# Wide feature maps and zero-weight filler matmuls in a kernel planned by its own scheduler

## The chip, the cores and the metric

The program runs on one core of a Trainium2 chip. Times are device microseconds of that core; the span that a profile shows, from the first to the last instruction, is some 2 us shorter.

## The reference

Four residual layers over 2048 tokens of width 512 with 32 heads of 16. Layers 0 and 2 are "memory layers": causal attention within four segments of 512 tokens, plus a linear-attention memory that runs over the segments. Layers 1 and 3 are plain attention over all 2048 tokens.

```python
phi = lambda t: jnp.where(t > 0, t + 1.0, jnp.exp(t))
for s in range(N):                                   # memory layer, N = 4 segments
    logits = jnp.einsum('bhqd,bhkd->bhqk', qs, ks) * scale + mask
    a_dot = jnp.einsum('bhqk,bhkd->bhqd', _softmax(logits, axis=-1), vs)
    pq = phi(qs)
    a_mem = jnp.einsum('bhld,bhde->bhle', pq, M) / (jnp.einsum('bhld,bhd->bhl', pq, z)[..., None] + 1e-06)
    outs.append(g * a_mem + (1.0 - g) * a_dot)
    pk = phi(ks)
    M = M + jnp.einsum('bhld,bhle->bhde', pk, vs)
    z = z + jnp.einsum('bhld->bhd', pk)
# ... layers: x + A(ln(x)), x + B(ln(x)), x + A(ln(x)), x + B(ln(x)); A = memory layer, B = full attention
```

Nearly all the work is the exponential of the softmax. Most of it runs on ACT (three 128x512 score tiles at a time, from three PSUM banks, while PE fills the three others). Some runs on DVE by a polynomial, four tiles at a time.

## The kernel before

The program is built by a planner in Python. It keeps a modelled time for each engine and puts down, step by step, what PE is to do next: a group of scores, a product with V, or a dense projection that some thread waits for. The order on every engine is fixed by this plan. Its numbers are tuned by stage: `TUNE` lists them by the count of exponentials planned so far, and `PAT` says how units of two layers are interleaved. The planner also models the PE clock. It counts activity in windows of 3.41 us and adds `CF * cold` to a matmul when it thinks the clock is half.

```python
def clock(self, t, work):                      # the planner's model of the PE clock
    w = int(t / HAM_W)                         # HAM_W = 3.4133
    if w > self.win:
        self.warm = w == self.win + 1 and self.work >= HAM_T     # HAM_T = 5.0
        self.win, self.work = w, 0.0
    self.work += work                          # 1.0 dense 512 columns, 0.14 a score tile, 0.16 a product with V
...
# end of the planning loop: PE has nothing ready until `to`
    if KEEP and self.acc_open and t + d <= tc + KEEP_D and (...) <= sc.lately() < KEEP and (...):
        self.keep_warm()                       # KEEP = 0.0 here: never
        continue
    sc.t["pe"] = to
...
# memory layers, one chunk of 512 columns at a time: masked query, feature map, masked query
sc.add("dve", lambda e: e.tensor_scalar(qe, qo, self.parm[:, 0:1], None, op0=ALU.mult), ...)
if L % 2 == 0 and s > 0:
    yield from self.g_phi(L, s, qo, self.b_q[z][1][c], self.ph[:, c, :], self.b_ph[c], f"q{c}")
o = sc.add("dve", lambda e: e.tensor_scalar(qo, qo, self.parm[:, 1:2], None, op0=ALU.mult), ...)
...
def g_phi(...):                                # phi(t) = max(t, 0) + min(exp(t), 1)
    o = sc.add("act", lambda e: e.activation(dst, src, ACT.Exp), ..., cost=0.65)
    o = sc.add("dve", lambda e: e.tensor_scalar(dst, dst, 1.0, None, op0=ALU.min), ..., cost=0.29)
    o = sc.add("dve", lambda e: e.scalar_tensor_tensor(res, src, 0.0, dst, op0=ALU.max, op1=ALU.add), ..., cost=0.71)
...
# layer norm of a segment: four tiles through two buffers, each transposed by a DMA
xn, bxn = self.xn[:, i % 2, :], self.b_xn[i % 2]
o = sc.add("dve", ... e.tensor_scalar(xn, xt, mu, r1, op0=ALU.subtract, op1=ALU.mult) ...)
o = self.dma_T(self.xT[:, s, :, i * 128:(i + 1) * 128], xn, [bxn], [self.b_xT[s][i]], f"lT{L}_{s}{i}")
```

The softmax here doesn't subtract the row's maximum and nothing guards it: scores larger than these inputs give would overflow.

## Time and profile before

| | before |
|---|---|
| time, median of the first 3 runs | 2082.6 us |
| ACT busy / PE busy / DVE busy | 96% / 82% / 79% |
| mean PE clock | 0.649 |
| ACT's own work (steps of its instructions, end to end) | 1976.3 us |
| ACT's loss up to the 110th exponential (191 us) | 44.4 us |
| loss from the 110th to the 1100th (191 to 1495 us) | 43.9 us |
| loss after that | 9.5 us |
| after ACT's last instruction | 8.1 us |

"Loss" is used throughout as in the prediction: the distance from the end of one ACT instruction to the end of the next, less that instruction's own step (1.343 us for 1536 columns from PSUM, 0.490 for 512, 0.515 for 512 from SBUF). Work, loss and the rest after the last instruction add up to the span. I call the three stretches start-up, middle and end. "Warm" and "cold" stand for the full and the half clock of PE.

The costliest groups of the page (line, engine, operation, tiles and shapes, count | busy us and mean ns | idle before it and what ended that idle) show the same bound from PE's side:

```profile
L1135 ACT ACTIVATE pT<-ps 128x1536 bf16<-128x1536 f32 (+2 forms) x1525 | 1957.3, 1458 | 66.1 <-PE ps L1128 57.4
L1128 PE MATMUL ps<-q,kB 32*128 32x512 bf16 x3660 | 699.6, 546 | 256.3 <-ACT pT L1135 248.3
```

PE waits 248 us for ACT to free banks ahead of its scores; ACT waits 57 us for scores.

### The profile page before, as it was taken

The numbers are of one execution on the slowest core, as the hardware profiler recorded it, in microseconds if no ns is written. First come the engines' busy times: TensorE is split into PE (matmuls) and PEld (weight loads), VectorE is DVE, ScalarE is ACT, GpSimd is POOL, SyncE is SP. The second block draws the span as 40 slices with busy tenths as digits, with TensorE's granted clock in tenths as the row PEclk, the third lists the DMA queues.
The fourth block names the chain that finished last, engine by engine and source line by source line (L and its number), as shares of the span: only waits on it lengthen the run. The fifth ranks groups of instructions, "written<-read, shape, count | busy, mean of one in ns | idle before, by whom it ended". The sixth has DMA issues, their size and how long they took to land.

```text
span 2082.3 us, 41423 instructions
## 1 busy us (share of the span) xinstructions
PE 1705.9 (82%) x17296; PEld 592.2 (28%) x17382; DVE 1645.9 (79%) x2492; ACT 1990.4 (96%) x1615; POOL 253.3 (12%) x564
## 2 busy tenths in 40 slices
PE   6768888888878888788787788888888888888887
PEld 2222221112311121212222223213444444444443
DVE  6886758887678688787878577688789988898986
ACT  6879899999999999999999999999999999999997
POOL 4542410001400000211013103100000000000000
PEclk9679897557565675557776797675655555555555
DMA  4210100001000000001010100100000000000000
GB/s 122 51 32 11 28 15 1 1 1 21 7 16 1 11 11 1 1 1 21 1 21 1 21 11 2 21 1 2 14 5 4 4 14 4 5 4 15 6 4 12
DMA packets 75467, 27.31 MB, mean 13 GB/s; under 512 B 68112, under 2 KB 74768, under 8 KB 75280
## 3 DMA queue, kind: packets, MB, share of 16 engines
q1 hardware_dynamic: 74176, 23.62, 5.2%
q8 instruction: 136, 2.23, 0.5%
q10 hardware_dynamic: 1104, 1.05, 0.2%
q14 instruction: 51, 0.42, 0.1%
HBM read 6.30 MB, written 2.10 MB: 4 GB/s over the span
## 4 chain that ended last, share of the span: by engine, by line
ACT 49%; PE 29%; issue 11%; DVE 7%; POOL 2%; DMA 1%; SPq 0%; ACTq 0%; DVEq 0%; POOLq 0%
ACT pT L1135 48%; PE ps L1128 13%; PE ps L625 6%; PE ps L1379 5%; PE ps L1397 4%; POOL pT L1158 2%; PE ps L1267 1%; DMA xT<-xn 1%; DVE lnst L662 1%; DVE T L1517 0%; DVE tokk L786 0%; ACT ph L780 0%; DVE ot L919 0%; SPq L444 0%; DVE db L1325 0%
## 5 line engine op out<-in xcount | busy, mean ns | idle before, releaser
L1135 ACT ACTIVATE pT<-ps 128x1536 bf16<-128x1536 f32 (+2 forms) x1525 | 1957.3, 1458 | 66.1 <-PE ps L1128 57.4
L1128 PE MATMUL ps<-q,kB 32*128 32x512 bf16 x3660 | 699.6, 546 | 256.3 <-ACT pT L1135 248.3
L1270 DVE TENSOR_SCALAR dz<-ps 128x512 int32<-128x512 f32 x436 | 301.0, 691 | 156.8 <-PE ps L1267 143.6
L1128 PEld LDWEIGHTS ps<-q,kB 32*128 32x128 bf16 x3660 | 131.4, 97 | 701.5 <-ACT pT L1135 656.1
L1158 POOL TENSOR_SCALAR_AFFINE_SELECT pT<-pT 128x256 bf16<-128x256 bf16 (+2 forms) x516 | 223.8, 463 | 613.4 <-ACT pT L1135 611.9
L1397 PE MATMUL ps<-pT,vB 128*17 128x512 bf16 x2216 | 278.7, 507 | 0.7 <-DVE q L640 0.5
L1267 PE MATMUL ps<-q,kB 32*128 32x512 bf16 x436 | 250.0, 573 | 0.0
L1379 PEld LDWEIGHTS ps<-vB,pT 128*128 128x128 bf16 x5776 | 181.1, 104 | 160.8 <-issue 157.6
L1379 PE MATMUL ps<-vB,pT 128*128 128x17 bf16 x5776 | 213.4, 177 | 0.7 <-ACT pT L1135 0.4
L1128 PE MATMUL ps<-q,kA 32*128 32x512 bf16 (+3 forms) x1024 | 122.4, 385 | 47.7 <-ACT pT L1135 45.6
L1307 DVE TENSOR_SCALAR df<-dz 128x2048 f16<-128x2048 uint16 x109 | 134.0, 1229 | 2.4
L1397 PEld LDWEIGHTS ps<-pT,vB 128*17 128x17 bf16 x2216 | 51.0, 89 | 187.0 <-issue 176.5
L1314 DVE TENSOR_SCALAR db<-dz 128x2048 int16<-128x2048 int16 x80 | 97.8, 1222 | 1.6 <-PE ps L1397 1.6
L1517 DVE STREAM_TRANSPOSE T<-ps 128x512 f32<-128x512 f32 x94 | 66.6, 709 | 15.3 <-PE ps L1397 14.7
L625 PE MATMUL ps<-xT,wB 128*128 128x512 bf16 x228 | 70.4, 429 | 7.4 <-issue 3.9
L625 PE MATMUL ps<-xT,wA 128*128 128x512 bf16 x238 | 68.7, 412 | 8.1 <-issue 2.1
L991 DVE TENSOR_TENSOR x_tok<-x_tok,ps 128x512 bf16<-128x512 bf16 x60 | 41.0, 686 | 41.6 <-PE ps L625 41.3
L1319 DVE TENSOR_TENSOR tokk<-tokk,df 128x2048 f16<-128x2048 f16 x58 | 70.7, 1219 | 0.7
L1323 DVE TENSOR_TENSOR tokk<-tokk,df 128x2048 f16<-128x2048 f16 x58 | 70.7, 1218 | 0.6
L1128 PEld LDWEIGHTS ps<-q,kA 32*128 32x128 bf16 x1024 | 29.9, 99 | 125.7 <-ACT pT L1135 110.9
L680 DVE TENSOR_SCALAR xn<-x_tok,lnmv,lnr 128x512 bf16<-128x512 bf16 x60 | 24.5, 429 | 50.3 <-DMA xT<-xn 49.4
L1325 DVE TENSOR_TENSOR db<-db,dz 128x2048 int16<-128x2048 int16 x51 | 62.8, 1231 | 1.2
(128 smaller groups left out, 1513.2 us busy)
## 6 DMA issues: line engine op xcount, KB each, us to landing
x_tok<-in_A_x_dram SPq DMA_DIRECT2D x14, 128.0 KB, 2.7
wB<-in_B_wqkv_dram SPq DMA_DIRECT2D x4, 384.0 KB, 3.9
out_dram<-x_tok SPq DMA_DIRECT2D x3, 512.0 KB, 3.0
xT<-xn SPq DMA_TRANSPOSE x60, 2.4
wA<-in_A_wk_dram SPq DMA_DIRECT2D x1, 512.0 KB, 7.7
wA<-in_A_wq_dram ACTq DMA_DIRECT2D x1, 512.0 KB, 7.9
wA<-in_A_wv_dram SPq DMA_DIRECT2D x1, 512.0 KB, 8.8
woA<-in_A_wo_dram SPq DMA_DIRECT2D x1, 512.0 KB, 7.5
```

What stands on the lines that cost most here:

```text
L625: return self.sc.add("pe", lambda e: e.matmul(out, lhsT, rhs, start=start, stop=stop), reads=reads, bank_ops=[(bank, "w", alloc)], emit=la ...
L1128: sc.add("pe", (lambda out, lhsT, rhs: lambda e: e.matmul(out, lhsT, rhs, start=True, stop=True))(out, lhsT, rhs), reads=reads, bank_ops=[ ...
L1135: o = sc.add("act", lambda e: e.activation(dst, src, ACT.Exp, scale=float(SCALE)), writes=[self.b_pT[s0 + i] for i in range(n)], bank_ops= ...
L1158: om = sc.add("pool", (lambda ap, pat: lambda e: e.affine_select(ap, ap, pattern=pat, compare_op=ALU.is_ge, fill=0.0, base=0, channel_mult ...
L1267: sc.add("pe", lambda e: e.matmul(out, lhsT, rhs, start=True, stop=True), reads=reads, bank_ops=[(bank, "w", alloc)], emit=True, name="SX" ...
L1270: o = sc.add("dve", lambda e: e.tensor_scalar(dst, out, float(EXP_C * 65536.0), -126.0 * 65536.0, op0=ALU.mult, op1=ALU.max), writes=[self ...
L1307: o = dv(lambda e: e.tensor_scalar(F, lo, 2.0 ** -16, -0.5, op0=ALU.mult, op1=ALU.add), bz, bF, "dF", 1.24)
L1314: o = dv(lambda e: e.tensor_scalar(E, hi, 128.0, 16256.0 + 53.0, op0=ALU.mult, op1=ALU.add), bz, bE, "dE", 1.24)
L1319: o = dv(lambda e: e.tensor_tensor(Pz, Pz, F, ALU.mult), bF + bP, bP, "dP2", 1.24)
L1323: o = dv(lambda e: e.tensor_tensor(Pz, Pz, F, ALU.mult), bF + bP, bP, "dP4", 1.24)
L1379: op = sc.add("pe", (lambda o0, w, v, first: lambda e: e.matmul(self.ps[:, o0:o0 + 17], w, v, start=first, stop=True, skip_group_check=Tru ...
L1397: sc.add("pe", (lambda out, v, rhs, start, stop: lambda e: e.matmul(out, v, rhs, start=start, stop=stop, skip_group_check=True))(out, v, r ...
```

## The change

Its intent: (1) where ACT is the bound, save fixed costs by mapping two chunks in one instruction; (2) where PE would idle, issue a matmul with zero weights that adds nothing, or one into a free bank that nobody reads, so that the PE clock stays at full speed and projections take half the time. New planner numbers and orders come with it.

```diff
-PAT = ["AAAAAAAA", "ABABABABBBABAAABBA", "BAAABBBAAAAA", "AAAAABABABAB", "AAAABABABBAA", "BBABAABAAA"]
+PAT = ["AAAAAAAA", "ABABABABBBABAAABBA", "BAAABAABABAA", "AAAAABABBBAA", "AAABBBABAAAA", "BBABABAAAA"]
+HALF = True
-    (0, {'CF': 0.829, 'PB': 0.02, 'DX_AHEAD': 0.5, ...}),
+    (0, {'CF': 1, 'PB': 0.026, 'DX_AHEAD': 0.696, ..., 'KEEP': 0.0, 'KEEP0': 3.0, 'KEEP_D': 0.0}),
+    (110, {'MMC': 0.205, 'KEEP': 9.0}),
     ... (all rows of TUNE are new)
+    (1100, {'DX_AHEAD': 0.664, 'MMC': 0.2, 'KEEP': 0.0, 'KEEP_D': 0}),
-        self.et = sb("et", [P, 512], bf)
+        self.et = sb("et", [P, 1024], bf)
+        if HALF and L % 2 == 0 and s > 0:
+            h = c // 2                       # waits for both chunks of the half, then
+            ...                              # mask, map (wide=True) and mask over 1024 columns
-            for c in range(NCH):
+            for h in range(2):
                 yield ("t", o.t_end, 0.0)
-                ... g_phi(L, s, tk, self.b_tokk[c], et, self.b_et, f"k{c}", tk, self.b_tokk[c])
+                tk = self.tokk[:, 2 * h:2 * h + 2, :].rearrange("p i f -> p (i f)")
+                ... g_phi(L, s, tk, self.b_tokk, self.et[:, :], self.b_et, f"k{h}", tk, self.b_tokk, wide=True)
-            if KEEP and self.acc_open and t + d <= tc + KEEP_D and (...) and self.pvu and self.pvu[0]["L"] <= KEEP_L:
-                self.keep_warm()
+            if KEEP and t + d <= tc + KEEP_D and (0.0 if sc.warm else KEEP0) <= sc.lately() < KEEP and self.keep_warm():
     def keep_warm(self):
+        if self.acc_open:
+            bank, alloc, start = self.acc_bank, self.acc_alloc, False
+        else:
+            bank = self.free_bank()
+            if bank.t_free + 0.12 > sc.t["pe"]:
+                return False
+            alloc, start = self.new_alloc(), True
+        sc.add("pe", lambda e: e.matmul(self.ps[:, bank.col0:bank.col0 + 512], self.zw[:, :], self.wA[:, 0, 0:512], start=start, stop=start,
+                                        skip_group_check=True), ..., name="D", cost=0.215, cold=0.2133, work=1.0)
+        return True
```

(Cut: a small constant tile now lives in the scratch buffer `et`.)

More of the change, by code (lines that the diff above doesn't have):

```diff
@@ L54 @@
 DX3 = 1
+HALF = True
 TUNE = [
-    (0, {'CF': 0.829, 'PB': 0.02, 'DX_AHEAD': 0.5, 'DX_SLACK': 4.776, 'DX_LEAD': 69, 'DVE_AHEAD': 4.525, 'MAXPV': 3, 'RATE': 0.606, 'MMC': 0.22, 'LN_G': 3, 'PV0': 0.371, 'DX3': 1}),
-    (110, {'CF': 0.849, 'RATE': 0.472, 'MMC': 0.229}),
-    (220, {'MMC': 0.213, 'PV0': 0.365}),
-    (330, {'LN_G': 2}),
-    (440, {'DVE_AHEAD': 2.5}),
-    (660, {'PB': 0.022}),
-    (880, {'PB': 0.026, 'RATE': 0.4}),
-    (990, {'MMC': 0.2, 'PV0': 0.324}),
-    (1100, {'CF': 1, 'PB': 0.025, 'DX_AHEAD': 0.676, 'LN_G': 3}),
-    (1210, {'PB': 0.036, 'DX_LEAD': 64, 'DVE_AHEAD': 3.61}),
-    (1320, {'DX_SLACK': 5.687}),
-    (1430, {'PB': 0.035, 'DX_LEAD': 53, 'DVE_AHEAD': 3.961, 'MAXPV': 2}),
+    (0, {'CF': 1, 'PB': 0.026, 'DX_AHEAD': 0.696, 'DX_SLACK': 4.776, 'DX_LEAD': 69, 'DVE_AHEAD': 4.525, 'MAXPV': 3, 'RATE': 0.581, 'MMC': 0.22, 'LN_G': 3, 'PV0': 0.371, 'DX3': 1, 'KEEP': 0.0, 'KEEP0': 3.0, 'KEEP_D': 0.0}),
+    (110, {'MMC': 0.205, 'KEEP': 9.0}),
+    (220, {'DX_LEAD': 64}),
+    (440, {'CF': 0.912, 'PB': 0.029}),
+    (550, {'DX_AHEAD': 0.5}),
+    (660, {'PB': 0.023, 'KEEP0': 1.467, 'KEEP_D': 0.003}),
+    (770, {'PB': 0.024, 'RATE': 0.679}),
+    (880, {'MAXPV': 4, 'KEEP_D': 0.03}),
+    (990, {'DX_AHEAD': 0.603, 'MMC': 0.207, 'KEEP0': 1.866}),
+    (1100, {'DX_AHEAD': 0.664, 'MMC': 0.2, 'KEEP': 0.0, 'KEEP_D': 0}),
+    (1210, {'PB': 0.02, 'DX_AHEAD': 0.749, 'DVE_AHEAD': 5.31, 'PV0': 0.368}),
+    (1320, {'CF': 1}),
+    (1430, {'DX_AHEAD': 1.301}),
 ]
@@ L346, in alloc @@
         self.gm = sb("gm", [P, NCH, 136], bf)
-        self.bmf = sb("bmf", [P, 136], f32)
+        self.bmf = self.et[:, 0:272].bitcast(f32)
         self.parm = sb("parm", [P, 2], f32)
@@ L397, in alloc @@
         self.b_gm = B("gm")
-        self.b_bmf = B("bmf")
+        self.b_bmf = self.b_et
         self.b_parm = B("parm")
@@ L769, in g_q @@
             return
+        if HALF and L % 2 == 0 and s > 0:
+            h = c // 2
+            key = ("cnt_q", L, s, h)
+            self.cnt[key] = self.cnt.get(key, 0) + 1
+            if self.cnt[key] < 2:
+                return
+            cs = slice(2 * h, 2 * h + 2)
+            qo, qe = self.q[:, z, 1, cs, :], self.q[:, z, 0, cs, :]
+            bo, be = self.b_q[z][1][cs], self.b_q[z][0][cs]
+            o = sc.add("dve", lambda e: e.tensor_scalar(qe, qo, self.parm[:, 0:1], None, op0=ALU.mult),
+                       reads=bo + [self.b_parm], writes=be, name=f"qm{L}{s}0", cost=0.45)
+            yield from self.g_phi(L, s, qo, bo, self.ph[:, cs, :], self.b_ph[cs], f"q{c}", wide=True)
+            o = sc.add("dve", lambda e: e.tensor_scalar(qo, qo, self.parm[:, 1:2], None, op0=ALU.mult),
+                       reads=bo + [self.b_parm], writes=bo, name=f"qm{L}{s}1", cost=0.45)
+            for x in (2 * h, 2 * h + 1):
+                self.set_ev(("q", L, s, x), o.t_end)
+            return
         sc.add("dve", lambda e: e.tensor_scalar(qe, qo, self.parm[:, 0:1], None, op0=ALU.mult),
@@ L776, in g_q, with g_phi @@
         self.set_ev(("q", L, s, c), o.t_end)
-    def g_phi(self, L, s, src, bsrc, dst, bdst, nm, res=None, bres=None):
+    def g_phi(self, L, s, src, bsrc, dst, bdst, nm, res=None, bres=None, wide=False):
         sc = self.sc
-        o = sc.add("act", lambda e: e.activation(dst, src, ACT.Exp), reads=[bsrc], writes=[bdst], name=f"phe{L}{s}{nm}", cost=0.65)
+        bsrc, bdst = ([x] if isinstance(x, Buf) else list(x) for x in (bsrc, bdst))
+        o = sc.add("act", lambda e: e.activation(dst, src, ACT.Exp), reads=bsrc, writes=bdst, name=f"phe{L}{s}{nm}", cost=1.07 if wide else 0.65)
         yield ("t", o.t_end, 0.0)
-        o = sc.add("dve", lambda e: e.tensor_scalar(dst, dst, 1.0, None, op0=ALU.min), reads=[bdst], writes=[bdst],
-                   name=f"phm{L}{s}{nm}", cost=0.29)
+        o = sc.add("dve", lambda e: e.tensor_scalar(dst, dst, 1.0, None, op0=ALU.min), reads=bdst, writes=bdst,
+                   name=f"phm{L}{s}{nm}", cost=0.43 if wide else 0.29)
         if res is None:
             res, bres = dst, bdst
-        o = sc.add("dve", lambda e: e.scalar_tensor_tensor(res, src, 0.0, dst, op0=ALU.max, op1=ALU.add), reads=[bsrc, bdst],
-                   writes=[bres], name=f"phs{L}{s}{nm}", cost=0.71)
+        o = sc.add("dve", lambda e: e.scalar_tensor_tensor(res, src, 0.0, dst, op0=ALU.max, op1=ALU.add), reads=bsrc + bdst,
+                   writes=bres if isinstance(bres, list) else [bres], name=f"phs{L}{s}{nm}", cost=1.24 if wide else 0.71)
         return o
@@ L862, in g @@
             self.set_ev(("phk", L, s))
-            for c in range(NCH):
+            for h in range(2):
                 yield ("t", o.t_end, 0.0)
-                tk = self.tokk[:, :, c * 128:(c + 1) * 128]
-                et = self.et[:, :].rearrange("p (i f) -> p i f", i=4)
-                o = yield from self.g_phi(L, s, tk, self.b_tokk[c], et, self.b_et, f"k{c}", tk, self.b_tokk[c])
+                tk = self.tokk[:, 2 * h:2 * h + 2, :].rearrange("p i f -> p (i f)")
+                o = yield from self.g_phi(L, s, tk, self.b_tokk, self.et[:, :], self.b_et, f"k{h}", tk, self.b_tokk, wide=True)
             for c in range(NCH):
@@ L1846, in run @@
             tc = min([x for x in (rs, rp, rx) if x is not None], default=to)
-            if KEEP and self.acc_open and t + d <= tc + KEEP_D and (0.0 if sc.warm else KEEP0) <= sc.lately() < KEEP and self.pvu and self.pvu[0]["L"] <= KEEP_L:
-                self.keep_warm()
+            if KEEP and t + d <= tc + KEEP_D and (0.0 if sc.warm else KEEP0) <= sc.lately() < KEEP and self.keep_warm():
                 continue
@@ L1857, in keep_warm @@
     def keep_warm(self):
-        bank = self.acc_bank
-        self.sc.add("pe", lambda e: e.matmul(self.ps[:, bank.col0:bank.col0 + 512], self.zw[:, :], self.wA[:, 0, 0:512], start=False, stop=False,
-                                             skip_group_check=True),
-                    reads=[self.b_zw, self.b_wA[0]], bank_ops=[(bank, "w", self.acc_alloc)], emit=False, name="D", cost=0.215, cold=0.2133, work=1.0)
+        sc = self.sc
+        if self.acc_open:
[6 more added lines that the diff above has]
+        sc.add("pe", lambda e: e.matmul(self.ps[:, bank.col0:bank.col0 + 512], self.zw[:, :], self.wA[:, 0, 0:512], start=start, stop=start,
+                                        skip_group_check=True),
+               reads=[self.b_zw, self.b_wA[0]], bank_ops=[(bank, "w", alloc)], emit=False, name="D", cost=0.215, cold=0.2133, work=1.0)
+        return True
     def ensure_any(self):
```

## The prediction

> **What bounds the kernel now.** I read the page's engine shares and slices first, then a table by stage, then ACT's waits, then two stretches of the timeline. ACT is the bound: 96% busy, above 9 tenths from the fifth slice on, and half of the chain that ended last is its exponentials.
>
> ```profile
> PE 1705.9 (82%) x17296; PEld 592.2 (28%) x17382; DVE 1645.9 (79%) x2492; ACT 1990.4 (96%) x1615; POOL 253.3 (12%) x564
> ...
> PE   6768888888878888788787788888888888888887
> ...
> ACT  6879899999999999999999999999999999999997
> ...
> PEclk9679897557565675557776797675655555555555
> ```
>
> "Busy" flatters ACT, because neighbours overlap. In the trace, where one instruction follows another without a gap, the ends lie 1.343 us apart for an exponential of 1536 columns, 0.916 for 1024, 0.490 for 512 (all read from PSUM), and 0.515 for the 512-column ones that read SBUF. So ACT's own work is 1254 x 1.343 + 267 x 0.916 + 4 x 0.49 = 1930.9, plus 48 SBUF-fed exponentials x 0.515 = 24.7, plus 36 copies x 0.49 = 17.6, plus about 3.4 of small things: 1976.6 us. The span is 2082.3. What can be won besides work is the 105.7 us in which ACT was short of work, 8 of them after its last instruction. Setting the distance of each pair of ends against these steps gives the loss by stage: 44.4 us up to 191 us (start-up, the first memory layer), 44.0 from 191 to 1495 us, 9.5 after that.
>
> In the table by stage (columns: stretch, its length, busy time and count of PE, PEld, DVE, ACT, POOL, then PEclk, DMA share, GB/s) look at PE against PEclk. From 260 to 310 us the clock is full, from 832 to 884 it is half, with PE equally busy. In the last stage PE is busy 153 of 182 us and still cold.
>
> ```profile
> 0.00:191.00 191.00, 140.41 (x1120) 46.27 (x1136) 148.69 (x339) 149.51 (x159) 92.18 (x219) 0.83 0.25 59
> 191.00:1495.00 1304.00, 1068.82 (x8760) 306.12 (x8820) 992.53 (x1551) 1269.57 (x1031) 161.15 (x345) 0.68 0.05 9
> 1495.00:2082.00 587.00, 496.64 (x7418) 239.83 (x7427) 504.64 (x603) 571.36 (x428) 0.00 (x0) 0.52 0.03 7
> 260.00:310.00 50.00, 41.77 (x313) 12.70 (x320) 28.43 (x53) 48.81 (x48) 7.53 (x18) 1.00 0.09 17
> 832.00:884.00 52.00, 41.07 (x398) 11.71 (x398) 37.06 (x55) 52.00 (x40) 13.75 (x32) 0.50 0.01 1
> 1508.00:1690.00 182.00, 153.31 (x2346) 74.57 (x2345) 163.79 (x194) 181.13 (x136) 0.00 (x0) 0.52 0.02 5
> ```
>
> A cold PE is no loss by itself: from 832 to 884 us ACT has no gap. The waits of ACT from 191 to 1495 us name what does cost, the score matmuls (L1128), 28 us in 40 waits:
>
> ```profile
> ACT pT L1135 <- PE ps L1128: 28.2, 40, 3.8
> ```
>
> The timeline shows how. The same four-matmul projection (L625) takes 1.04 us at the full clock and 1.89 at half, between score groups that ACT needs every 1.34 us. While warm, ACT runs nine exponentials in a row; after each cold one it has a gap (0.49, 0.69).
>
> ```profile
> 958.21 1.04 PE L625 MATMUL ps<-xT,wB 128*128 128x512 bf16 x4
> ...
> 967.57 1.89 PE L625 MATMUL ps<-xT,wB 128*128 128x512 bf16 x4
> ...
> 971.43 1.89 PE L625 MATMUL ps<-xT,wB 128*128 128x512 bf16 x4
> ```
> ```profile
> 957.46 12.20 ACT L1135 ACTIVATE pT<-ps 128x1536 bf16<-128x1536 f32 x9
> 970.15 2.96 ACT L1135 ACTIVATE pT<-ps 128x1536 bf16<-128x1536 f32 x2 [0.49 <-PE ps L1128]
> 973.80 1.45 ACT L1135 ACTIVATE pT<-ps 128x1536 bf16<-128x1536 f32 x1 [0.69 <-PE ps L1128]
> ```
>
> I sorted the 44.0 us of the middle stage by the clock granted 0.6 us before each ACT instruction: 35.6 us fall on 624 instructions under the half clock, 8.3 on 405 under the full one, and 6.0 of those 8.3 before 333 us. From 333 to 1495 us it is 33.2 against 2.3. This is what makes me believe in the change.
>
> **What the Trainium skill says.** "TensorE: Matmul & The Clock Gate", section "What's actually happening": the gate knows a half and a full state, decided over free-running windows of about 3.4 us. The trace agrees: the clock records are 0.5 or 1.0 only, in multiples of 3.413 us. The same page's section "Why this matters for your kernels" asks for PE to be busy for 4 us and to have no idle gaps; here the trace differs, as PE is 84% busy in the last stage at a clock of 0.52. Matmuls that fill 32 rows or 17 columns of the array evidently count little, so a dense matmul is the right filler. Its section "Back-to-back issue gap" gives N/1.2 ns cold and N/2.4 + 2.5 ns warm, so 427 and 216 ns for 512 columns; the pairs 1.89 and 1.04 us above fit (three gaps of 427 or 216 plus one latency). "Perfetto Trace Analysis", section "Optimizing Scalar/DVE Operations": a Scalar instruction has about 93 ns of access overhead on SBUF and 51 on PSUM. The trace has 515 - 427 = 88 ns and 490 - 427 = 63 ns; I use these.
>
> **The change part by part.** I counted instructions in the two built programs.
> *Wide feature maps and masks.* On ACT 48 exponentials of 512 become 24 of 1024: 24 x 88 ns = 2.1 us less. On DVE 48 masks (0.365 us) become 24; from 0.365 at 512 and 0.751 at 2048 columns I estimate 0.494 at 1024, so 24 x 0.236 = 5.7 us less. The minimum (0.315) and the max-add (0.70) save by the same reasoning about 4.4 and 4.1 us. DVE is 79% busy, so its 14 us count only where its chain is waited for: the start-up, where ACT idled 4.1 us at the key feature map with its single scratch buffer (two rounds now in place of four). Against it, the first chunk's masked queries are ready only with the second's.
> *ACT's remaining work, from the new order.* Score tiles left to ACT fall from 4300 to 4292 (two more groups of four go to DVE, 444 against 436). The exponentials become 1239 x 1.343 + 285 x 0.916 + 5 x 0.49 = 1927.5 us, 3.4 less. Copies fall from 36 to 30: 2.9 us less. With the 2.1 this is **8.4 us** of ACT work, nearly all on the path, as ACT is the bound.
> *DVE* takes 8 more tiles at 0.69 and 2 more chains at about 7.5 us, and 6 copies: about 25 us more, less 14 saved. It stays under 82%.
> *Zero-weight matmuls.* 526 of 128x512, none before, all between the 110th and 1100th exponential (about 191 to 1495 us). Warm, by the skill's 216 ns, they are an estimate of 114 us of PE time; PE stood idle 248 us ahead of score matmuls waiting for ACT, so there is room. Are there enough? The kernel's scheduler counts a score tile 0.14, a product with V 0.16 and a dense matmul 1.0, and wants 5 in a window. At 1.34 us per three tiles a window holds 7.6 tiles, so about 2.3; 2.7 fillers are missing per window, and 526 supply 195. Half clock in this stage is 2 x (1 - 0.68) x 1304 = 835 us, 245 windows. So I expect the clock of the stage to go from 0.68 to about 0.9. The fillers are thin between the 384th and 512th group of three score tiles (8 of 526), so that part stays cold.
> If four fifths of the cold time turns warm and loses at the warm rate, the 35.6 us shrink to about 7 + 5 = 12. Some of it waits for a transposing DMA or a DVE chain and would be lost at any clock (3.75 us at 1148 us is the greatest), and some fillers will come badly: I count **18 us** won of 24.
> *Start-up.* New order, no fillers: **4 us** won, give or take 6. *After 1495 us:* fillers off, 9.5 us of loss stay.
> Sum: 8.4 + 18 + 4 = 30; 2082.6 - 30 = about **2053 us**.
>
> **The rivals.**
> *A, warmth buys nothing.* ACT's loss sits with cold windows only because a burst of projections meets an engine still cold and then warms it; or zero weights don't count as activity. Then only work and start-up count: about 2072. For it: the coldest stages lose least (1.3 us from 772 to 916 us). Against: the 1.04 against 1.89 us above.
> *B, the fillers stand in the way.* 474 of 526 stand straight ahead of a score group and 19 runs of them carry a wait for DVE. A cold filler is 427 ns; a tenth of a microsecond lost at each is 50 us, so 2110. Against it: a score group has the 1.34 us of the other half's exponential as slack and needs 0.39 warm or 0.61 cold.
> *C, all the loss of the middle goes and start-up gains 8 us:* 2082.6 - 8.4 - 35 - 8 = 2031. For it: warm stretches from 333 us on lose 2.3 us in 292 instructions. Against: dependencies don't vanish.
> *D, DVE becomes what is waited for,* through 8 more tiles and wider steps: some 5 to 10 us given back, inside the range.
>
> **Range and chances.** 2072 of A and 2036, near C, bound the likely; the range is 2036 to 2073 us. Faster by over 2% means under 2040.9 us, 41.7 us won: only if nearly all the loss of the middle goes, 0.20. Slower needs B at full strength: 0.02. Within 2%: 0.78.
>
> **What would show it.** Right: PEclk of 191 to 1495 us near 0.9 and its ACT waits for score matmuls under 12 us; after 1495 us all as it was; ACT's exponentials at the same steps, work down 8 us. Projections of 512 columns there in 1.04 us. Wrong if: the clock rises and the waits stay (A), the clock doesn't rise (zero weights don't count), score groups are late behind L1885 (B), or start-up moves by more than 10 us. The prediction as a whole fails most easily by the share of the cold loss that is really a dependency.

## More of the kernel before

What follows goes by ratios with their 95% intervals, and by one profiled run of each kernel.

## The result, and the profile after

The changed kernel took 2068.3 us (median of 4 runs, 2067.9 to 2070.8) against 2081.0 (4 runs, 2078.9 to 2085.5) for the kernel before in the same rounds. The ratio is 0.9939, with a 95% interval from 0.9919 to 0.9958. Ratios here are the mean time of one kernel's runs over that of the other's in the same rounds, so not quite the ratio of the medians. About 13 us were won where 30 were predicted.

From the page after: the engine shares, the slices of ACT and of the clock, and the three groups that answer to those before.

```profile
PE 1759.0 (85%) x17908; PEld 621.4 (30%) x17908; DVE 1653.7 (80%) x2448; ACT 1981.3 (96%) x1589; POOL 266.1 (13%) x563
...
ACT  6779999999999999999999999999999999999998
...
PEclk9779899868556995579958997795655555555555
...
L1154 ACT ACTIVATE pT<-ps 128x1536 bf16<-128x1536 f32 (+2 forms) x1529 | 1949.0, 1446 | 63.6 <-PE ps L1147 56.3
L1147 PE MATMUL ps<-q,kB 32*128 32x512 bf16 x3652 | 656.1, 508 | 204.5 <-ACT pT L1154 186.3
...
L1885 PE MATMUL ps<-wA,zw 128*128 128x512 bf16 x526 | 165.1, 395 | 0.0
```

The 526 fillers took PE's idle time: its wait for ACT ahead of scores fell from 248 to 186 us. Their mean of 395 ns says that nearly all ran warm; in the trace 501 have the full-clock duration, 25 the half-clock one. But what ACT waited for scores in all has hardly moved (57.4 and 56.3 us). By stage (columns as in the prediction's table):

```profile
0.00:192.00 192.00, 142.58 (x1148) 47.24 (x1149) 146.22 (x315) 145.33 (x144) 98.76 (x219) 0.85 0.27 59
192.00:1487.00 1295.00, 1132.54 (x9403) 339.32 (x9401) 1009.64 (x1536) 1268.67 (x1017) 167.31 (x344) 0.80 0.05 9
1487.00:2066.00 579.00, 483.91 (x7359) 234.89 (x7359) 497.86 (x598) 567.28 (x432) 0.00 (x0) 0.52 0.03 7
```

The middle's clock rose from 0.68 to 0.80, and the end's is as it was. ACT's waits in the middle (total, number, longest):

```profile
ACT pT L1154 <- PE ps L1147: 20.1, 34, 2.3
```

| us, profiled runs | before | after | change | predicted |
|---|---|---|---|---|
| ACT's work | 1976.3 | 1968.1 | -8.2 | -8.4 |
| loss, start-up | 44.4 | 48.9 | +4.5 | -4 |
| loss, middle | 43.9 | 35.2 | -8.7 | -18 |
| loss, end | 9.5 | 7.1 | -2.4 | 0 |
| after ACT's last instruction | 8.1 | 7.5 | -0.6 | 0 |
| span | 2082.3 | 2066.8 | -15.5 | -30 |

So two terms are wrong: the start-up by 8.5 us and the middle by 9.3. Of the signs that the prediction named for being right, the clock of the middle (near 0.9) and ACT's waits there (under 12 us) didn't come; the steps of ACT's instructions and its work did.

The start-up lost in two gaps, each over 9 us. The timeline of the first, from DVE to PE to ACT, and ACT's line of the second:

```profile
84.85 0.41 DVE L682 TENSOR_SCALAR xn<-x_tok,lnmv,lnr 128x512 bf16<-128x512 bf16 x1 [2.48 <-DMA xT<-xn]
86.29 0.41 DVE L682 TENSOR_SCALAR xn<-x_tok,lnmv,lnr 128x512 bf16<-128x512 bf16 x1 [1.03 <-DMA xT<-xn]
...
86.97 0.64 PE L627 MATMUL ps<-vA,tokk 128*128 128x136 bf16 x4 [4.39 <-DVE M_sb L900]
...
93.71 1.45 ACT L1154 ACTIVATE pT<-ps 128x1536 bf16<-128x1536 f32 x1 [9.83 <-PE ps L1147]
...
153.76 2.42 ACT L1154 ACTIVATE pT<-ps 128x1024 bf16<-128x1024 f32 x2 [13.62 <-PE ps L1147]
```

DVE's third and fourth normalised tile wait for the DMA that transposes the first two out of the buffers. Behind them in the planned order stand the memory's copies out of PSUM; PE waits 4.4 us for one of those, with the next scores behind it. In the kernel before, ACT's longest single wait in this stretch, past the first 20 us, was 6.2 us.

### The profile page after: what moved, and what is told of

Read it like the earlier page. It is cut to its first block, busy times and chain, and to the rows that moved or that the text cites. A ratio compares the mean times of both kernels' runs of the same rounds, so it can differ in the third digit from the quotient of the medians.

```text
span 2066.8 us, 42473 instructions
## 1 busy us (share of the span) xinstructions
PE 1759.0 (85%) x17908; PEld 621.4 (30%) x17908; DVE 1653.7 (80%) x2448; ACT 1981.3 (96%) x1589; POOL 266.1 (13%) x563
## 4 chain that ended last, share of the span: by engine, by line
ACT 51%; PE 29%; issue 12%; DVE 4%; POOL 2%; DMA 1%; SPq 0%; ACTq 0%; DVEq 0%; POOLq 0%
ACT pT L1154 50%; PE ps L1147 12%; PE ps L627 6%; PE ps L1398 5%; PE ps L1416 4%; POOL pT L1177 2%; PE ps L1286 1%; DMA xT<-xn 1%; PE ps L1885 1%; DVE lnst L664 0%; DVE T L1536 0%; SPq L446 0%; DVE ph L806 0%; DVE ot L938 0%; ACT ph L800 0%
## 5 line engine op out<-in xcount | busy, mean ns | idle before, releaser
L1154 ACT ACTIVATE pT<-ps 128x1536 bf16<-128x1536 f32 (+2 forms) x1529 | 1949.0, 1446 | 63.6 <-PE ps L1147 56.3
L1147 PE MATMUL ps<-q,kB 32*128 32x512 bf16 x3652 | 656.1, 508 | 204.5 <-ACT pT L1154 186.3
L1289 DVE TENSOR_SCALAR dz<-ps 128x512 int32<-128x512 f32 x444 | 305.3, 690 | 154.2 <-PE ps L1286 140.1
L1177 POOL TENSOR_SCALAR_AFFINE_SELECT pT<-pT 128x256 bf16<-128x256 bf16 (+2 forms) x515 | 235.6, 489 | 526.4 <-ACT pT L1154 524.5
L1416 PE MATMUL ps<-pT,vB 128*17 128x512 bf16 x2208 | 248.7, 450 | 3.9 <-DVE dz L1289 1.3
L1286 PE MATMUL ps<-q,kB 32*128 32x512 bf16 x444 | 240.2, 541 | 0.0
L1885 PE MATMUL ps<-wA,zw 128*128 128x512 bf16 x526 | 165.1, 395 | 0.0
L1536 DVE STREAM_TRANSPOSE T<-ps 128x512 f32<-128x512 f32 x94 | 66.7, 709 | 12.8 <-PE ps L1416 11.9
L627 PE MATMUL ps<-xT,wB 128*128 128x512 bf16 x256 | 74.4, 419 | 1.3 <-DMA xT<-xn 0.7
L627 PE MATMUL ps<-xT,wA 128*128 128x512 bf16 x256 | 70.1, 401 | 6.2 <-DMA xT<-xn 2.1
L672 POOL TENSOR_SCALAR lnr<-lnmv 128x4 f32<-128x4 f32 x15 | 4.9, 328 | 532.9 <-DVE lnmv L667 530.0
```

The costliest lines, as they stand in the source:

```text
L627: return self.sc.add("pe", lambda e: e.matmul(out, lhsT, rhs, start=start, stop=stop), reads=reads, bank_ops=[(bank, "w", alloc)], emit=la ...
L1147: sc.add("pe", (lambda out, lhsT, rhs: lambda e: e.matmul(out, lhsT, rhs, start=True, stop=True))(out, lhsT, rhs), reads=reads, bank_ops=[ ...
L1154: o = sc.add("act", lambda e: e.activation(dst, src, ACT.Exp, scale=float(SCALE)), writes=[self.b_pT[s0 + i] for i in range(n)], bank_ops= ...
L1177: om = sc.add("pool", (lambda ap, pat: lambda e: e.affine_select(ap, ap, pattern=pat, compare_op=ALU.is_ge, fill=0.0, base=0, channel_mult ...
L1286: sc.add("pe", lambda e: e.matmul(out, lhsT, rhs, start=True, stop=True), reads=reads, bank_ops=[(bank, "w", alloc)], emit=True, name="SX" ...
L1289: o = sc.add("dve", lambda e: e.tensor_scalar(dst, out, float(EXP_C * 65536.0), -126.0 * 65536.0, op0=ALU.mult, op1=ALU.max), writes=[self ...
```

## The experiments

Fourteen kernels ran; all gave the reference's result. Experiments "in the same order" have every other instruction in the sequence of the kernel that they start from. Where the planner ran anew, that is said, and it matters.

### What the fillers are worth

The planner's decisions stay, but the fillers are not emitted; their waits are.

```diff
+            if op.name == "D":
+                assert not op.emit
+                continue
             ins = op.fn(eng_obj)
```

> The changed kernel with its 526 zero-weight matmuls left out of the program, all else in the same order and with the same waits. Theory W (the fillers keep PE warm, and that shortens ACT's waits from 191 to 1495 us): the clock of that stretch falls from 0.79 to about 0.65, ACT's loss there rises from 35 us to 45-55, the whole takes 2078-2088 us, ratio to the kernel before 0.998 to 1.003. Rival P (the gain of the middle came from the new plan and order, not from the clock): clock falls, loss stays near 35 us, 2065-2070 us, ratio about 0.993. Rival B (the fillers stand in the way): faster than with them, under 2064 us.

Measured: 2092.6 us, ratio 1.0045 (1.0032 to 1.0059). The middle's clock was 0.67 and its loss 61.6 us. Theory W held, and by more than it said: the fillers are worth 1.0045 - 0.9939 = 1.06%, some 22 us where I had predicted 18 for them (the two ratios come from different rounds, and their intervals leave some 5 us either way). But the new order without them loses 17.7 us more in the middle than the old order (61.6 against 43.9). One stretch in both kernels, around the 686th exponential; first the changed kernel's PE (L1885 are fillers, L627 an output projection) and ACT:

```profile
951.51 0.60 PE L1885 MATMUL ps<-wA,zw 128*128 128x512 bf16 x2
952.03 1.04 PE L627 MATMUL ps<-woB,oT 128*128 128x512 bf16 x4
953.00 0.39 PE L1147 MATMUL ps<-q,kB 32*128 32x512 bf16 x3
...
954.18 1.04 PE L627 MATMUL ps<-woB,oT 128*128 128x512 bf16 x4
```
```profile
953.55 7.74 ACT L1154 ACTIVATE pT<-ps 128x1536 bf16<-128x1536 f32 x6 [0.28 <-PE ps L1147]
```

Then the same projections without fillers (L630):

```profile
967.35 1.89 PE L630 MATMUL ps<-woB,oT 128*128 128x512 bf16 x4
...
970.79 1.89 PE L630 MATMUL ps<-woB,oT 128*128 128x512 bf16 x4
```
```profile
966.08 2.37 ACT L1157 ACTIVATE pT<-ps 128x1536 bf16<-128x1536 f32 x2 [1.78 <-PE ps L1150]
969.94 2.79 ACT L1157 ACTIVATE pT<-ps 128x1536 bf16<-128x1536 f32 x2 [1.50 <-PE ps L1150]
973.53 1.45 ACT L1157 ACTIVATE pT<-ps 128x1536 bf16<-128x1536 f32 x1 [0.79 <-PE ps L1150]
```

A projection every 2 us at 1.04 us each fits between ACT's groups; at 1.89 it doesn't, and ACT stands for 0.8 to 1.8 us.

### Is it the clock?

All 526 fillers, 16 columns wide in place of 512.

```diff
-        ... self.ps[:, bank.col0:bank.col0 + 512], self.zw[:, :], self.wA[:, 0, 0:512] ...
+        ... self.ps[:, bank.col0:bank.col0 + 16], self.zw[:, :], self.wA[:, 0, 0:16] ...
```

> The changed kernel with all 526 fillers 16 columns wide in place of 512: they take an instruction's place on PE and its weight load, but hardly any activity. Theory W (what counts is the clock): clock of the middle stretch 0.65-0.68, 2089-2096 us, as without fillers, ratio 1.003-1.006. Rival I (their standing between the instructions helps by something else): under 2080 us.

Measured: 2096.1 us, ratio 1.0068 (1.0055 to 1.0081), middle's clock 0.68, its loss 63.7 us. As without fillers (the intervals overlap): what helps is the activity and the clock that it brings, not the place that a filler takes in the order.

### Would more warmth win more?

In the changed kernel's order, fillers are added at no modelled cost, also where the clock is cold and where the idle time is up to 0.25 us too short.

```diff
+FREE, FREE_0, FREE_N, FREE_GAP = (110, 1100), 0.0, 8, 0.25
...
+            if FREE[0] <= len(self.log) < FREE[1]:
+                self.free_fill(t, tc)        # up to FREE_N fillers, cost 0 in the model, while t + d <= tc + FREE_GAP
             sc.t["pe"] = to
```

> The changed kernel in the same order with 989 zero-weight matmuls in place of 526: also with a cold clock, and where the planner's idle time is up to 0.25 us too short for one. Theory F (the fillers were too few: the middle stretch is warm for 0.80 only, and its cold third loses 54 ns per ACT instruction as before): clock over 0.9, ACT's loss from 192 to 1487 us from 35 to 18-25 us, whole 2054-2062 us, ratio 0.986-0.990. Rival Q (what is left are dependencies, or the added fillers stand in the way): clock over 0.9, loss 33 us or more, whole 2066 us or more, ratio 0.993 or more.

Measured: 2074.8 us, ratio 0.9963 (0.9950 to 0.9976): no gain over 526 fillers, and rather a loss, though the intervals just overlap. The middle of the profiled run:

```profile
192.00:1490.00 1298.00, 1182.18 (x9867) 368.25 (x9865) 1009.46 (x1538) 1271.00 (x1016) 166.01 (x344) 0.88 0.05 9
```

The clock rose to 0.88 (over 0.9 was expected), and the loss went from 35.2 to 38.1 us. Theory F fell and rival Q held. The loss under the half clock stayed (21.0 us, then 21.7), although only 219 ACT instructions in place of 392 fell on it. Q names two causes for that, dependencies or fillers in the way. The table at the end of the next experiment tells them apart.

### The same in the old order

Twice, the kernel before in its own order, with fillers where its planner sees PE idle: first 321 of them (gap allowance 0), then 809 (0.2 us).

> The kernel before, its order unchanged, with 321 zero-weight matmuls put where its planner sees PE idle, between the 110th and the 1100th exponential. Theory W: clock of 191 to 1495 us from 0.68 to 0.75-0.8, ACT's loss there from 44 us to 30-37, whole 2070-2077 us, ratio 0.994-0.998. Rival P: clock rises, loss stays at 42-46 us, ratio 0.999-1.001. Rival B: slower, ratio over 1.002.

Measured: 2082.1 us, ratio 0.9993 (0.9980 to 1.0006); middle's clock 0.74, loss 42.4 us. Its shorter start-up (41.6 us of loss) has the same instructions as the kernel before, so some 3 us of that stretch is spread from run to run. Rival P held by its numbers.

> The kernel before in its own order with 809 zero-weight matmuls between the 110th and the 1100th exponential; 321 of them raised the clock from 0.68 to 0.74 and won nothing sure. Theory F: clock of 191 to 1495 us over 0.85, loss there from 44 to under 30 us, whole 2062-2070 us, ratio 0.990-0.994. Rival R (the old order's waits are mostly dependencies that come with a cold clock and aren't caused by it): clock over 0.85, loss 38-46 us, ratio 0.997-1.003.

Measured: 2091.1 us, ratio 1.0046 (1.0033 to 1.0058). The middle:

```profile
189.00:1501.00 1312.00, 1153.92 (x9630) 359.56 (x9628) 991.30 (x1550) 1271.38 (x1031) 161.60 (x345) 0.87 0.05 9
```

The clock went from 0.68 to 0.87 and the loss from 43.9 to 52.2 us; 41.6 of it fell on the 232 instructions under the half clock, where 35.5 had fallen on 624. This was neither theory: not F, and worse than R.

The totals suggest that ACT's loss isn't the clock's doing. That reading is wrong. The order is kept, so each ACT instruction can be compared with itself. Around the 859th exponential in the kernel before, PE with a cold projection (the record of its fourth matmul is missing from the trace) and ACT:

```profile
1190.12 1.48 PE L625 MATMUL ps<-xT,wB 128*128 128x512 bf16 x3 [0.33 <-issue]
```
```profile
1192.31 6.96 ACT L1135 ACTIVATE pT<-ps 128x1536 bf16<-128x1536 f32 x5 [1.50 <-PE ps L1128]
```

The same place with 809 fillers: the projection is warm and ACT's gap is gone.

```profile
1198.73 1.04 PE L649 MATMUL ps<-xT,wB 128*128 128x512 bf16 x4
```
```profile
1192.58 14.54 ACT L1159 ACTIVATE pT<-ps 128x1536 bf16<-128x1536 f32 x11
```

But 147 of the 809 fillers ran cold themselves, as here ahead of scores (L1152):

```profile
1115.70 1.89 PE L1891 MATMUL ps<-wA,zw 128*128 128x512 bf16 x4
1117.52 0.61 PE L1152 MATMUL ps<-q,kB 32*128 32x512 bf16 x3
...
1118.29 1.45 ACT L1159 ACTIVATE pT<-ps 128x1536 bf16<-128x1536 f32 x1 [1.34 <-PE ps L1152]
```

All ACT instructions of the middle, sorted by the clock granted 0.6 us before each in the two kernels, and those that stayed cold by whether a cold filler ran in the 3 us before them (1.5 or 6 us in place of 3 give a like picture). Each cell has the number of instructions and their loss in us, first and then:

| clock, first and then | new order: no filler, then 526 | new order: 526, then 989 | old order: no filler, then 809 |
|---|---|---|---|
| warm, warm | 351: 11.2, 8.8 | 609: 14.2, 13.7 | 387: 5.4, 4.8 |
| cold, warm | 272: 32.2, 5.4 | 187: 7.7, 2.7 | 410: 19.9, 5.8 |
| cold, cold, no cold filler ahead | 330: 16.0, 16.9 | 98: 10.3, 9.8 | 74: 13.6, 14.1 |
| cold, cold, behind a cold filler | 43: 1.5, 2.0 | 107: 3.0, 11.3 | 140: 2.1, 21.4 |
| warm, cold | 19: 0.7, 2.0 | 14: 0.0, 0.6 | 18: 3.0, 6.1 |

In both orders, where warmth arrived most of the loss went. This isn't slack from a new wait just before: in the last column the 211 of the 410 with no wait grown in the 20 instructions ahead of them went from 10.4 to 3.1 us. What grew in the crowded kernels stands behind fillers that ran cold: 25 of the 526, 92 of the 989, 147 of the 809. The 321 fillers of the smaller test show the first half too (123 instructions turned warm: 10.5 us, then 1.7; 501 stayed cold: 25.1, then 30.9), but 74 of its filler records are missing from the trace. So more warmth did win, and what was lost behind cold fillers used it up. This is read from matched traces; a run that leaves out the cold fillers alone wasn't made.

Dependencies that no clock shortens are there too: the wait of 3.9 us at the 827th exponential, which the prediction named, is in the kernel before and in both of these.

### Which fillers matter?

The changed kernel in the same order, with fillers emitted only between the 110th and 220th and the 660th and 990th exponential, where leaving them out had cost most (251 of them), or only in the rest (275).

```diff
+ONLY = [(110, 220), (660, 990)]
-                   ..., name="D", ...
+                   ..., name="D" if any(a <= len(self.log) < b for a, b in ONLY) else "D0", ...    # "D0" isn't emitted
```

> The changed kernel, same order and waits, with the 251 fillers between the 110th and 220th and the 660th and 990th exponential alone (the stretches where leaving all of them out raised ACT's loss, by 6.2 and 17.8 us); the other 275 are left out of the program. Theory L (a filler is worth something only where dense projections stand close together; elsewhere a cold PE costs ACT nothing): 2066-2071 us, ratio 0.993-0.995, loss of the left-out stretches 16-18 us. Rival E (each filler is worth about the same, 24 us over 526): 2078-2082 us, ratio about 0.999.

> The other 275 fillers alone, between the 220th and 660th and the 990th and 1100th exponential. Theory L: 2088-2093 us, ratio 1.002-1.005, as with none. Rival E: 2078-2082 us.

Measured: 2073.0 us, ratio 0.9963 (0.9951 to 0.9975), and 2082.1 us, ratio 1.0001 (0.9989 to 1.0013). Against 1.0045 without any, the first half won 0.8% and the other 0.4%. L missed both numbers, E missed the first and all but met the second: L is right in tendency, but the other half isn't worthless. In the trace without fillers the chosen stretches have 694 weight loads of the line that issues projections over 440 exponentials, the rest 306 over 550.

### The start-up

In the changed kernel, two spare buffers take the third and fourth normalised tile of the first layer. The planner's times stay as with two buffers, so the order is unchanged.

```diff
+            if L == 0 and i >= 2:
+                xn, bxn = self.db[:, i - 2, :], self.b_dbx[i - 2]
...
+                       soft=[self.xn_dma[i % 2]] if L == 0 and self.xn_dma[i % 2] else [])   # counts in the model, is no wait
```

> The changed kernel in the same order; in the first layer the third and fourth normalised tile of a segment go to other buffers, so that DVE needn't wait for the transposing DMA of the first two. Theory D (the two great gaps of ACT in the start-up, 9.8 us at 94 and 13.6 us at 154 us, are DVE held in order behind that DMA): the gaps shrink by 3 us each, whole 2060-2064 us, ratio 0.990-0.992. Rival C (the alternation of PE and DVE after it sets the gaps): under 1.5 us won, ratio 0.993-0.994.

Measured: 2064.1 us, ratio 0.9911 (0.9897 to 0.9925). PE's wait for the memory's copy and ACT's two gaps:

```profile
82.55 0.63 PE L629 MATMUL ps<-vA,tokk 128*128 128x136 bf16 x4 [0.77 <-DVE M_sb L906]
```
```profile
89.30 2.37 ACT L1160 ACTIVATE pT<-ps 128x1536 bf16<-128x1536 f32 x2 [6.22 <-PE ps L1153]
```
```profile
149.11 2.42 ACT L1160 ACTIVATE pT<-ps 128x1024 bf16<-128x1024 f32 x2 [10.23 <-PE ps L1153]
```

PE's wait was 4.39 us and is 0.77. Each gap shrank by about 3.5 us, as theory D says (the second by 2.8 against the 13.0 us that it lasts in four other runs of this order); 2.8 us came back in a new wait at 99 us, so the stretch's loss fell from 48.9 to 44.6. The rest of the gaps is something else.

Is it the long instructions or the order around them? Each wide map or mask is issued as two half-width instructions in the same place.

```diff
-        o = sc.add("act", lambda e: e.activation(dst, src, ACT.Exp), ...)
+        o = sc.add("act", lambda e: two(lambda d, s_, r: e.activation(d, s_, ACT.Exp)), ...)    # columns 0:512, then 512:1024
```

> The changed kernel in the same order, each wide map or mask issued as two half-width instructions in the same place. By the prediction's prices ACT has 2.1 us more work and DVE some 14. Theory O (the order around the wide steps makes the start-up's two great gaps): both gaps stay at 9-11 and 13-15 us, whole 2069-2074 us, ratio 0.994-0.997. Rival Z (the length of the wide instructions makes them): gaps under 6 and 10 us, whole 2062-2067 us.

Measured: 2069.6 us, ratio 0.9941 (0.9929 to 0.9954); ACT's work 2.1 us up, as priced; the gaps 9.8 and 12.8 us, the second just under what O said. Theory O held: the order makes them. The width itself is worth no more than the noise: 0.02% of the ratio.

### Parts alone, planned anew

The wide maps with the old planner numbers and order strings; narrow maps in layer 0 with the new ones; narrow maps in both layers.

> The wide maps and masks alone: the new code with the kernel before's order strings and planner numbers, no fillers. My prediction's step (start-up wins some us): 2074-2080 us, ratio 0.996-0.999, ACT's loss before 191 us under 44 us. Theory S (the wide maps lengthen the start-up, because the key maps and the masked queries of a segment come later): loss before 191 us at 47-50 us, whole 2081-2086 us, ratio 1.000 to 1.002.

> The changed kernel with one-chunk maps and masks in the first memory layer, wide ones in the third layer alone; its planner runs anew. Theory S (wide maps cost the start-up about 4.5 us): ACT's loss before 191 us falls from 49 to 43-46 us; ACT's own work 1 us up; whole 2063-2068 us, ratio 0.990-0.993. Rival T (the start-up's loss came from the new planner numbers): loss there stays at 48-50 us, ratio 0.993-0.996.

> The changed kernel without the wide maps and masks, in both memory layers; fillers and planner numbers stay, the planner runs anew and places 759 fillers. If the wide maps are worth their 2.1 us of ACT work and cost the start-up 4.5 us, this takes 2064-2068 us; if they carry the new plan, over 2072 us.

Measured: 2100.8 us (ratio 1.0090), 2104.2 (1.0101) and 2101.9 (1.0088). On the start-up alone they agree with theory S: with wide maps its loss is 49.0 us under the old numbers as under the new (gaps of 9.7 and 14.9 us), and with narrow ones 45.3 and 46.9 (no gap over 7.7 past the first 20 us). But in the middle they lost 62, 72 and 68 us, against 43.9 and 35.2 in the two kernels whose numbers belong to their plan.

> The changed kernel with fillers switched off in the planner, which then plans anew without them, the other new numbers and the order strings kept. Theory K (the new order loses 61.6 us in the middle stretch without fillers because it was planned counting on a warm PE): loss there 44-52 us, whole 2076-2084 us, ratio 0.997-1.001. Rival N (the new numbers and order strings as such, or any plan they weren't tuned for): loss there 58 us or more, whole 2089 us or more, ratio 1.003 or more.

Measured: 2110.1 us, ratio 1.0133 (1.0119 to 1.0147), with a loss in the middle of 81.4 us. Rival N held, and theory K fell. All four kernels whose planner ran anew with numbers not searched for that case took 2101 to 2110 us. Such a run doesn't measure the part that it changes.

### To beat both

The spare buffers with the 251 fillers alone. (The text below says "planned anew"; in fact it was planned as the spare-buffer kernel above, with the old modelled waits, which is why the order is the same.)

> To beat both kernels: free buffers for the first layer's third and fourth normalised tile, planned anew with the true waits (the order of instructions turned out the same), and the 251 fillers alone. If both gains hold: 2061-2067 us, ratio 0.990-0.993. If theory E holds it is slower than the changed kernel, over 2072 us.

Measured: 2070.6 us, ratio 0.9946 (0.9933 to 0.9959): a miss, since the other 275 fillers are worth something. The best kernel is the spare-buffer one with all fillers, 2064.1 us. It beats the kernel before by 0.9%; over the changed kernel it is 4 us, which were measured in different rounds and whose intervals overlap.

## Why the prediction was wrong

**The bound and ACT's work were right.** ACT is the bound before and after, the steps of its instructions held, and its work fell by 8.2 us where 8.4 were worked out.

**The step that failed in the middle** is the supply of warmth: "2.7 fillers are missing per window, and 526 supply 195" of 245 windows, and so "If four fifths of the cold time turns warm". The clock rose from 0.68 to 0.80 only. Against the same order without fillers the half clock fell from 873 to 530 us, by 100 windows; that is 5.2 fillers for each. 131 of the 526 stood where the clock was full without them too, by the ACT instruction that follows each; 25 ran cold. The other 370 are still 3.7 to a window.

The other half of that sentence, "loses at the warm rate", held. The 272 instructions that turned warm lose 5.4 us, 20 ns each, just the warm rate of the kernel before (8.3 us over 405). By this rate four fifths of 624 instructions lose 10 us, not the "5" of the sum. Taken with the prediction's two rates (57 and 20 ns) the counts after, 392 cold and 623 warm, give 35 us of loss, and 35.2 were measured: by this sum the share of the cold time that turned accounts for the miss. That it fits so closely is partly luck, as the next term shows.

The share of the loss that is a dependency, the prediction's own caution, is real as well. One such wait in the changed kernel:

```profile
475.77 1.02 PE L627 MATMUL ps<-xT,wA 128*128 128x512 bf16 x4 [2.08 <-DMA xT<-xn]
```
```profile
477.28 1.45 ACT L1154 ACTIVATE pT<-ps 128x1536 bf16<-128x1536 f32 x1 [2.10 <-PE ps L1147]
```

The projection runs at full clock, yet ACT loses 2.1 us, for the transposing DMA came late.

**A term was missing from the sum:** the price of the new order itself. The new order without fillers loses 17.7 us more in the middle than the old one; the fillers then won 26.4 (61.6 to 35.2, the same order). The difference is the 8.7 us seen. The prediction had neither term, only their net. Why the new order loses more without them isn't settled: theory K, that it was planned for a warm PE, fell with a plan made without fillers that lost still more.

**The start-up had the wrong sign.** "4 us won, give or take 6" came from the key map's chain of four rounds becoming two. With the wide maps the plan has two gaps of over 9 us, with narrow maps none over 7.7, and some 3 us of each is DVE held behind a DMA. Shown are the gaps' dependence on the order (they stay with half-width instructions) and the DMA's share; the rest of the gaps, and why the planner orders so, stay open.

**Rivals.** A (warmth buys nothing) is wrong in both orders; in the old one, what was lost behind cold fillers cancelled what the warmth won. B (fillers in the way) didn't decide the changed kernel, where 25 ran cold, but did the crowded ones. C didn't come, nor D in the middle, where no wait of PE for DVE is over 1.6 us. The 2.4 us less in the end stretch, which has no fillers, came with the new order and is left unexplained.

## What to carry to other kernels

When a remedy leaves a total unchanged, keep the order and compare instruction by instruction before you say that it doesn't work: a gain where the clock turned full and a loss behind fillers that ran at half can cancel. Put a filler where it finds the clock full or turns it: the changed kernel's planner asks for some recent activity (`KEEP0`) before it adds one to a cold window, the crowded ones asked for none. Fillers paid most where dense projections stand close together. In a kernel whose order comes from a tuned planner, test a part with the order frozen; a fresh plan with foreign numbers took 18 to 28 us more than the kernel before, against 2 us of ACT work that the wide maps save.

## What the Trainium skill lacked or had wrong

- "TensorE: Matmul & The Clock Gate", section "Why this matters for your kernels", asks for a PE that is busy for 4 us and then has no idle gap over about 3 us. For matmuls like these it doesn't say what counts as busy. In the end stretch PE is busy 484 of 579 us with no gap over 0.9 us, yet the clock is 0.52, with matmuls of 32 rows or 17 columns. 526 dense fillers of 512 columns raised the middle from 0.67 to 0.80, and of 16 columns to 0.68.
- No page says whether matmuls with all-zero weights count as activity for the clock gate. They do: the same 526, with zero weights and a moving operand that isn't zero.
- "ScalarE: Activation LUTs", section "What ACT_TABLE_LOAD costs", gives an ACTIVATE 186 ns + 0.833 ns per column with an overlap of about 93 ns, which works out at 93 ns of fixed cost between neighbours, and doesn't tell PSUM from SBUF. The trace has 63 ns when reading PSUM and 88 ns when reading SBUF. "Perfetto Trace Analysis", section "Optimizing Scalar/DVE Operations", does tell them apart and is nearer, with 51 and 93 ns.
